# Attention probabilities of two heads handled together: the row shift, the cast and where they stand in each engine's queue

## The chip, the cores and the metric

The kernel runs on one core of a Trainium2 chip. A core has five engines that work side by side, each through its own queue and strictly in order: TensorE (PE in the profile, its weight loads PEld), VectorE (DVE), ScalarE (ACT), GpSimd (POOL) and SyncE (SP), which here only issues DMAs. The metric is the device time of one execution in microseconds (us), the median of several runs.

## The reference

The input x is 2048 rows of 576. Each row is normalised (`_layernorm`), and two branches use the result xn. The first is causal attention with a window of 256 over 32 heads of 18 columns each:

```python
qkv = (xn @ wqkv)                       # 3 x 32 heads x 18
scores = einsum("bhqd,bhkd->bhqk", q, k) * (18 ** -0.5)
mask = (0 <= q_index - k_index) & (q_index - k_index < 256)
p = softmax(where(mask, scores, -1e9))
s = einsum("bhqk,bhkd->bhqd", p, v) @ wo
```

The second is a bilinear gated block without a nonlinearity inside: g = silu(((xn @ w_gate) * (xn @ w_up)) @ w_down), with an inner width of 4608. The output is x + s * g.

## The kernel before, in words

All products are made in float16 with a high part and a low part: a value v becomes hi = f16(v) and lo = f16(v - hi), and two or three products of the parts replace one. That holds for the attention probabilities too: `probs` makes the high part and `turn_probs` the low one.

A first stage of some 185 us normalises x and makes q, k and v. The long middle stage, from there to about 1540 us, is a loop over 72 slots of 16 places each; a slot is one of 18 groups of 256 inner columns times one of 4 chunks of 512 rows. In every place TensorE makes a quarter of a gate or up product (L896 to L900). Everything else is hung on places by a list written out by hand, `at(slot, place, function)`: at each place the functions are called after the matmuls of the quarter, score products first, then down products, then the others in the order in which they were put on the list. This order is the order in each engine's queue. Places count on past 15 into the next slot, so place 18 of a slot is place 2 of the next.

Step s of the attention (64 of them, four row chunks c by 16 pairs of heads) lives in slot s + 1 and some places of the next. It has four blocks i of 128 rows, and two heads j. `score_pairs` (L647) makes the score tiles of two blocks, at places 3 and 11, into four banks of PSUM. Then, for each block and head:

- `score`: DVE reads the scores from PSUM, adds the mask, writes them to `sm` and takes the row maximum (L655, shown in the trace as a custom instruction and a read of its accumulator). POOL turns the maximum into the shift, mx * sig + shift, with one small instruction per head (L657).
- `probs`, two places later: ACT takes exp with a scale `sig` and the shift, both read from memory (L662), and casts the result to float16 into `pp` (L665).
- `turn_probs`, two more places later: the low part sm - hi is made by DVE for head 0 and by POOL for head 1 (L670). With head 1 the pair is complete, and SP issues one DMA that transposes `pp` into `pt` (L673).
- `weigh` (L682): TensorE multiplies `pt` with v.

For the first 16 steps (c = 0) the blocks i = 0, 1, 2, 3 have 128, 256, 384, 384 columns of scores per head, later ones 384 throughout.

The other users of DVE in a slot, in the order of the queue: the eviction of each half tile of the down product, `down` (L770 on PE, then L775 on DVE). There are eight of them in a slot, at places 7, 9, 11, 13, 15, 17, 19 and 21, and all use the one bank `dn`, so that a product can start only when the one before it is evicted. Then `up_out` (L747), `h_lo` (L757), the low parts of the weights `up_lo` and `dn_lo` (both L150), and the maxima of the raw weights (L356). At place 12 of every slot stands `finish` of the step before (its place 28): DVE divides the attention output (L694, L696, L698), and POOL casts it and makes its low part (L702, L706). GpSimd also makes a third, scaled copy of the down weights, `dn_low` (L394), twice in four slots.

The low parts of the weights at place 13, between the evictions of places 13 and 15, stand in two of every four slots (`up_lo` at 45 and `dn_lo` at 61, counted from the start of the group).

Of the kernel before, what the change touches and what calls it, by code (L numbers as in the profile page):

```python
# [8 lines left out]
F32 = mybir.dt.float32  # L9
FR = mybir.dt.float32r  # L10
BF = mybir.dt.bfloat16
F16 = mybir.dt.float16
AF = mybir.ActivationFunctionType
OP = mybir.AluOpType
# [6 lines left out]
def kernel(  # L21
# [10 lines left out]
    nc = tc.nc  # L32
# [12 lines left out]
    scale = DH ** -0.5  # L45
    shift = 14.0 * math.log(2.0)
# [11 lines left out]
    G_SC, U_SC, LO = 2.0 ** -27, 2.0 ** -17, 2.0 ** 11  # L58
# [27 lines left out]
    sig = const.tile([128, 4], F32, name="sig")  # L86
# [304 lines left out]

    def dn_low(g, k):
        w = DW[g, k]
        nc.gpsimd.tensor_scalar(w[:, 2], w[:, 0], 1.0 / LO, None, op0=OP.mult)  # L394


    def v_store(t):
# [35 lines left out]
    a, b = TB.pop(0)  # L433
# [87 lines left out]
    for t in range(16):  # L521
# [17 lines left out]
        elif t in (3, 5):  # L539

            k = (t + 5) // 2 - 1
# [11 lines left out]
        for m in range(QM):  # L553
            for c in (2 * half, 2 * half + 1):
# [6 lines left out]
                if half == 1:  # L561
                    if m in (1, 2, 3):
                        ffn_amax(0, m - 1, c - 2)
                    if m >= QM - 2:
                        k = 2 * (m - QM + 2) + c - 2
# [36 lines left out]
    att = att_stack.enter_context(tc.tile_pool(name="att", bufs=1))  # L602
    bias = att.tile([128, 384], BF, name="bias")
# [5 lines left out]
    QS, KS, VT, SP, SM, PP, PT, PVB, OB = {}, {}, {}, {}, {}, {}, {}, {}, {}  # L609
# [27 lines left out]
    def first_kb(s):  # L637
        return 2 if s < 16 else 0
# [11 lines left out]
    def score(s, j, i):  # L650
        ps = SP.pop((s, j, i))
        n = (i + 3 - max(first_kb(s), i)) * 128
        sm = att.tile([128, 384], F32, name="sm_", bufs=4)
        mx = att.tile([128, 2], F32, name="mx", bufs=3)
        nc.vector.tensor_tensor_reduce(sm[:, 384 - n:], ps[:, :n], bias[:, 384 - n:], 1.0, -3e38,  # L655
                                       op0=OP.add, op1=OP.max, accum_out=mx[:, 0:1])
        nc.gpsimd.tensor_scalar(mx[:, 1:2], mx[:, 0:1], sig[:, 1:2], shift, op0=OP.mult, op1=OP.add)  # L657
        SM[s, j, i] = (sm[:, 384 - n:], mx, n)

    def probs(s, j, i):  # L660
        sm, mx, n = SM[s, j, i]
        nc.scalar.activation(sm, sm, AF.Exp, bias=mx[:, 1:2], scale=sig[:, 0:1])  # L662
        if j == 0:
            PP[s, i] = att.tile([128, 1536], F16, name="pp", bufs=3)
        nc.scalar.copy(PP[s, i][:, 2 * n * j:2 * n * j + n], sm)  # L665

    def turn_probs(s, j, i):
        sm, mx, n = SM.pop((s, j, i))
        pp, a = PP[s, i], 2 * n * j
        (nc.gpsimd if j else nc.vector).tensor_tensor(pp[:, a + n:a + 2 * n], sm, pp[:, a:a + n], op=OP.subtract)  # L670
        if j == 1:
            pt = PT[s, i] = att.tile([128, 12, 128], F16, name="pt", bufs=3)
            nc.sync.dma_start(pt[:, 0:4 * n // 128], PP.pop((s, i))[:, 0:4 * n], transpose=True)  # L673

    def weigh(s, j, i):
        if (j, i) == (0, 0):
# [40 lines left out]
    def at(slot, place, f, *a):  # L717
        todo.setdefault(slot * 16 + place, []).append((f, a))

    first_slot = 1  # L720
    for s in range(NSTEP):
        b = first_slot + s
        at(b - 1, 5, load_k, s)
        at(b - 1, 9, load_q, s)
        at(b - 1, 13, load_v, s)
        at(b, 3, score_pairs, s, 0)
        at(b, 11, score_pairs, s, 2)
        for n in range(8):
            i, j = divmod(n, 2)
            p = (3, 4, 6, 8, 11, 12, 14, 16)[n]  # L730
            at(b, p, score, s, j, i)
            at(b, p + 2, probs, s, j, i)
            at(b, p + 4, turn_probs, s, j, i)
            at(b, 15 + 4 * i + (j if i < 3 else 0), weigh, s, j, i)
        at(b, 28, finish, s)
        if s % 16 == 15:
            for i in range(4):
                at(b, 33 + 4 * i, store_o, s // 16, i)
# [38 lines left out]
    for g in range(NG):  # L777
        b = 4 * g - 4
        if g > 0:
            for kind in range(3):  # L780
                for part in range(2):
                    at(b, ((0, 1, 2, 6, 10, 14) if g == 1 else (-6, -2, 2, 6, 10, 14))[2 * kind + part],
                       ffn_raw, g, kind, part)
                for half in range(2):
                    at(b, ((9, 13) if g == 1 else (5, 9), (17, 21), (24, 26))[kind][half], ffn_amax, g, kind, half)
            at(b, 28, ffn_spread_out, g)
            at(b, 34, ffn_spread_in, g)
            at(b, 41, ffn_scale, g)
            for k, (ph, pl) in enumerate(((42, 45), (47, 49), (51, 53), (55, 57))):
                at(b, ph, up_hi, g, k)  # L790
                at(b, pl, up_lo, g, k)
        for k, (ph, pw, pl) in enumerate(((60, 62, 61), (64, 66, 66)) if g else ((64, 65, 66), (68, 69, 70))):
            at(b, ph, dn_hi, g, k)
            at(b, pw, dn_low, g, k)
            at(b, pl, dn_lo, g, k)
# [89 lines left out]
    for sl in range(NSLOT + 1):  # L885
        g, c = divmod(sl, NCH)
        for place in range(16):
            if sl < NSLOT:
                k, quarter = divmod(place, 4)
                up, w = k % 2, UW[g, k]  # L890
# [3 lines left out]
                for i in range((13 * quarter + 3) // 4, (13 * (quarter + 1) + 3) // 4):  # L894
                    a, b = pl[i]
# [44 lines left out]
```

## Time and profile before

| quantity | value |
|---|---|
| median of 3 runs | 1655.34 us (1654.82 to 1655.62) |
| profiled execution, first to last instruction | 1651.6 us |
| granted TensorE clock, mean | 1.000 |
| busy PE / DVE / ACT / POOL | 1638.3 / 1185.1 / 913.6 / 596.2 us |
| share of the chain that ended last: PE | 93% |

The profiled execution gives only the span between its first and its last instruction; the difference to the median, 3.7 us, is what lies around it. A row of the timeline gives the start and the duration in us, the engine, the line, the operation, and what is written and read; in brackets is the idle time of the engine before it and who ended it. On one engine the next instruction often starts some 0.08 us before the end that is shown for the one before it. Where a duration per instruction is wanted as a step in a queue, the distance from start to start is therefore the right one. A row of the groups gives count, total busy time, mean in ns, and idle time before.

### The profile page before, as it was taken

Reading aid. Unit: us, or ns where it says so; the run is one execution under the profiler, and the core shown is the slowest. Engines: PE = TensorE matmul, PEld = TensorE weight load, DVE = VectorE, ACT = ScalarE, POOL = GpSimd, SP = SyncE. Lnnn points to the kernel's source line nnn. Section 1 sums busy time; section 2 is a strip of 40 time slices with the busy share of each in tenths; the row PEclk is TensorE's granted clock in tenths of the full one; section 3 lists DMA queues with packets and bytes.
Section 4 is the critical chain, followed back from the end, with each engine's and each line's share of the span. In section 5 each row is a group of like instructions: output and inputs, shape, how many; then the busy total and the mean of one; then the engine's idle time right before and its main releaser. Section 6 shows DMA issues by size and latency. Waiting matters only on the chain.

```text
span 1651.6 us, 33875 instructions
## 1 busy us (share of the span) xinstructions
PE 1638.3 (99%) x12307; PEld 933.2 (56%) x12307; DVE 1185.1 (72%) x2985; ACT 913.6 (55%) x1578; POOL 596.2 (36%) x1043
## 2 busy tenths in 40 slices
PE   8999999999999999999999999999999999999999
PEld 5464455555555555555555555555555555555577
DVE  7533577777777878787878777878787787865544
ACT  6431465656565666676666666665666666632230
POOL 3110134445343535454444444444444443511000
PEclk9999999999999999999999999999999999999999
DMA  9482445455556766665666575757665656650228
GB/s 239 134 216 90 116 84 115 90 114 104 114 106 132 142 124 135 109 146 112 145 135 142 105 147 105 151 105 145 138 135 113 140 116 129 126 123 28 60 69 219
DMA packets 535079, 206.39 MB, mean 125 GB/s; under 512 B 473856, under 2 KB 513664, under 8 KB 534912
## 3 DMA queue, kind: packets, MB, share of 16 engines
q1 hardware_dynamic: 534912, 204.23, 57.8%
q8 instruction: 97, 1.59, 0.4%
q14 instruction: 70, 0.57, 0.1%
HBM read 76.63 MB, written 23.75 MB: 61 GB/s over the span
## 4 chain that ended last, share of the span: by engine, by line
PE 93%; DMA 3%; DVE 1%; SPq 1%; POOL 1%; issue 1%; ACT 0%; POOLq 0%; ACTq 0%
PE up L896 47%; PE dn L770 25%; PE up L323 5%; PE pv L682 4%; PE up L899 3%; PE s L647 2%; DMA pt<-pp 2%; PE s L860 2%; PE up L860 1%; PE s L291 1%; PE s L770 1%; PE up L291 1%; SPq L337 1%; DMA xr<-in_A_x_dram 0%; SPq L238 0%
## 5 line engine op out<-in xcount | busy, mean ns | idle before, releaser
L896 PE MATMUL up<-XT,upw 128*128 128x512 f16 x3744 | 926.8, 378 | 0.0
L770 PE MATMUL dn<-dnw,hh 128*128 128x288 f16 x3360 | 504.5, 286 | 0.0
L896 PEld LDWEIGHTS <-upw 128*128 128x128 f16 x3744 | 331.1, 97 | 279.6 <-issue 0.6
L775 DVE SCALAR_TENSOR_TENSOR acc<-dn,sc,acc 128x288 f32<-128x288 f32 x528 | 272.2, 516 | 285.9 <-PE dn L770 285.8
L770 PEld LDWEIGHTS <-hh 128*128 128x128 f16 x3456 | 326.1, 98 | 199.0 <-issue 41.1
L657 POOL TENSOR_SCALAR mx<-mx,sig 128x1 f32<-128x1 f32 x512 | 193.5, 378 | 551.3 <-DVE mx L655 526.2
L682 PEld LDWEIGHTS <-pt 128*128 128x128 f16 x2880 | 137.3, 96 | 62.9 <-DMA pt<-pp 5.2
L682 PE MATMUL pv<-vt,pt 128*128 128x37 f16 x2880 | 143.0, 179 | 2.9 <-DMA pt<-pp 2.9
L742 ACT ACTIVATE gt<-up 128x512 f32<-128x512 f32 x144 | 85.4, 593 | 84.5 <-PE up L899 81.4
L752 ACT ACTIVATE hh<-ht 128x512 f16<-128x512 f32 x144 | 89.9, 624 | 61.5 <-DVE ht L747 61.5
L747 DVE SCALAR_TENSOR_TENSOR ht<-up,gt 128x512 f32<-128x512 f32 x144 | 99.0, 688 | 16.6 <-PE up L896 6.6
L757 DVE SCALAR_TENSOR_TENSOR hh<-hh,ht 128x512 f16<-128x512 f16 x144 | 98.7, 685 | 0.0
L323 PE MATMUL up<-XT,upw 128*128 128x512 f16 x448 | 97.0, 379 | 0.0
L356 DVE TENSOR_REDUCE am<-raw 128x1 f32<-128x640 f32 (+1 forms) x108 | 85.0, 787 | 3.0 <-DMA raw<-in_B_w_gate_dram 3.0
L394 POOL TENSOR_SCALAR dnw<-dnw 128x576 f16<-128x576 f16 x36 | 69.1, 1921 | 23.0 <-ACT dnw L147 20.3
L147 ACT ACTIVATE upw<-raw,sc 128x640 f16<-128x640 f32 x72 | 59.2, 824 | 26.1 <-DVE sc L126 26.1
L323 PEld LDWEIGHTS <-upw 128*128 128x128 f16 x448 | 43.8, 98 | 52.5
L328 DVE SCALAR_TENSOR_TENSOR qp<-up,qp 128x512 f16<-128x512 f32 x36 | 24.7, 685 | 59.4 <-ACT qp L327 42.7
L150 DVE SCALAR_TENSOR_TENSOR upw<-raw,sc,upw 128x640 f16<-128x640 f32 x72 | 63.1, 876 | 0.1
L647 PE MATMUL s<-ks,qs 54*128 54x384 f16 (+2 forms) x512 | 60.2, 312 | 0.0
L327 ACT ACTIVATE qp<-up 128x512 f16<-128x512 f32 x36 | 21.4, 597 | 66.6 <-PE up L323 56.1
L899 PE MATMUL up<-XT,upw 64*128 64x512 f16 x144 | 55.7, 387 | 0.0
(2227 smaller groups left out, 2123.1 us busy)
## 6 DMA issues: line engine op xcount, KB each, us to landing
raw<-in_B_w_down_dram SPq DMA_DIRECT2D x36, 288.0 KB
raw<-in_B_w_gate_dram SPq DMA_DIRECT2D x36, 256.0 KB
raw<-in_B_w_up_dram SPq DMA_DIRECT2D x36, 256.0 KB
qk_d<-qp SPq DMA_DIRECT2D x112, 72.0 KB
vt<-v_d SPq DMA_DIRECT2D x48, 111.0 KB
ks<-qk_d SPq DMA_DIRECT2D x96, 54.0 KB
v_d<-vo SPq DMA_DIRECT2D x16, 296.0 KB
xr<-in_A_x_dram SPq DMA_DIRECT2D x16, 288.0 KB
```

The source lines that it names most:

```text
L323: nc.tensor.matmul(ps, a, b, start=i == 0, stop=i == len(pl) - 1)
L647: nc.tensor.matmul(ps[:, :hi_ - lo_], QS[s][r, i * 128:(i + 1) * 128], KS[s][r, lo_:hi_], start=True, stop=True)
L657: nc.gpsimd.tensor_scalar(mx[:, 1:2], mx[:, 0:1], sig[:, 1:2], shift, op0=OP.mult, op1=OP.add)
L682: nc.tensor.matmul(PVB[s][:, j, i, :VW], pt[:, 2 * nb * j + n], VT[s][:, lo_ + n % nb, j * VW:(j + 1) * VW], start=n == 0, stop=n == 2 * n ...
L742: nc.scalar.activation(g, ps, AF.Copy, scale=G_SC)
L747: nc.vector.scalar_tensor_tensor(h, ps, U_SC, GT.pop((sl, ft)), op0=OP.mult, op1=OP.mult)
L752: nc.scalar.activation(hh[:, 0], h, AF.Copy, scale=1.0 / LO)
L757: nc.vector.scalar_tensor_tensor(hh[:, 1], hh[:, 0], -LO, h, op0=OP.mult, op1=OP.add)
L770: nc.tensor.matmul(ps[:, :HALF], a, b, start=q == 0, stop=q == len(l) - 1)
L775: nc.vector.scalar_tensor_tensor(d, ps[:, :HALF], SC[g][:, 9:10], d, op0=OP.mult, op1=OP.add)
L896: nc.tensor.matmul(banks[up], a, b, start=i == 0 and not up, stop=i == 12 and up == 1)
L899: nc.tensor.matmul(banks[0], *half_pass(w, c, False), start=False, stop=True)
```

## The change

For each block, both heads now share one `sm` and one `mx` tile. The DVE instruction multiplies by -C (the value `sig[:, 1:2]`, read from memory) while it adds the mask, and takes the minimum in place of the maximum, so that its accumulator already holds the scaled shift without its constant. POOL adds the constant for both heads with one instruction. `probs` and `turn_probs` are called once per block, at the places that head 1 had: two exps with the constant scale -1, one cast for both heads, then both low parts and the transposition. So head 0's exp, cast and low part move: its low part on DVE from places 7, 10, 15 and 18 to 8, 12, 16 and 20. The pools have three buffers of two heads where `sm` had four of one. The third copy of the down weights is written with a second operation, a multiplication by 1.0.

```diff
-        nc.gpsimd.tensor_scalar(w[:, 2], w[:, 0], 1.0 / LO, None, op0=OP.mult)
+        nc.gpsimd.tensor_scalar(w[:, 2], w[:, 0], 1.0 / LO, 1.0, op0=OP.mult, op1=OP.mult)
...
     def score(s, j, i):
-        sm = att.tile([128, 384], F32, name="sm_", bufs=4)
-        mx = att.tile([128, 2], F32, name="mx", bufs=3)
-        nc.vector.tensor_tensor_reduce(sm[:, 384 - n:], ps[:, :n], bias[:, 384 - n:], 1.0, -3e38,
-                                       op0=OP.add, op1=OP.max, accum_out=mx[:, 0:1])
-        nc.gpsimd.tensor_scalar(mx[:, 1:2], mx[:, 0:1], sig[:, 1:2], shift, op0=OP.mult, op1=OP.add)
+        if j == 0:
+            SM[s, i] = (att.tile([128, 2, 384], F32, name="sm_", bufs=3), att.tile([128, 4], F32, name="mx", bufs=3), n)
+        sm, mx, n = SM[s, i]
+        nc.vector.tensor_tensor_reduce(sm[:, j, :n], ps[:, :n], bias[:, 384 - n:], sig[:, 1:2], 3e38,
+                                       op0=OP.add, op1=OP.min, accum_out=mx[:, j:j + 1])
+        if j == 1:
+            nc.gpsimd.tensor_scalar(mx[:, 2:4], mx[:, 0:2], 1.0, shift, op0=OP.mult, op1=OP.add)
 
-    def probs(s, j, i):
-        nc.scalar.activation(sm, sm, AF.Exp, bias=mx[:, 1:2], scale=sig[:, 0:1])
-        nc.scalar.copy(PP[s, i][:, 2 * n * j:2 * n * j + n], sm)
+    def probs(s, i):
+        for j in range(2):
+            nc.scalar.activation(sm[:, j, :n], sm[:, j, :n], AF.Exp, bias=mx[:, 2 + j:3 + j], scale=-1.0)
+        PP[s, i] = att.tile([128, 2, 2, 384], F16, name="pp", bufs=3)
+        nc.scalar.copy(pp_of(s, i)[:, :, 0], sm[:, :, :n])
 
-    def turn_probs(s, j, i):
-        (nc.gpsimd if j else nc.vector).tensor_tensor(pp[:, a + n:a + 2 * n], sm, pp[:, a:a + n], op=OP.subtract)
-        if j == 1:
-            nc.sync.dma_start(pt[:, 0:4 * n // 128], PP.pop((s, i))[:, 0:4 * n], transpose=True)
+    def turn_probs(s, i):
+        for j in range(2):
+            (nc.gpsimd if j else nc.vector).tensor_tensor(pp[:, j, 1], sm[:, j, :n], pp[:, j, 0], op=OP.subtract)
+        nc.sync.dma_start(pt[:, 0:4 * n // 128], PP.pop((s, i)).rearrange("p j k n -> p (j k n)")[:, 0:4 * n], transpose=True)
...
             at(b, p, score, s, j, i)
-            at(b, p + 2, probs, s, j, i)
-            at(b, p + 4, turn_probs, s, j, i)
+            if j == 1:
+                at(b, p + 2, probs, s, i)
+                at(b, p + 4, turn_probs, s, i)
```

More of the change, by code (lines that the diff above doesn't have):

```diff
@@ L652, in score @@
         n = (i + 3 - max(first_kb(s), i)) * 128
-        sm = att.tile([128, 384], F32, name="sm_", bufs=4)
-        mx = att.tile([128, 2], F32, name="mx", bufs=3)
-        nc.vector.tensor_tensor_reduce(sm[:, 384 - n:], ps[:, :n], bias[:, 384 - n:], 1.0, -3e38,
-                                       op0=OP.add, op1=OP.max, accum_out=mx[:, 0:1])
-        nc.gpsimd.tensor_scalar(mx[:, 1:2], mx[:, 0:1], sig[:, 1:2], shift, op0=OP.mult, op1=OP.add)
-        SM[s, j, i] = (sm[:, 384 - n:], mx, n)
@@ L660, in probs @@
-    def probs(s, j, i):
-        sm, mx, n = SM[s, j, i]
-        nc.scalar.activation(sm, sm, AF.Exp, bias=mx[:, 1:2], scale=sig[:, 0:1])
-        if j == 0:
-            PP[s, i] = att.tile([128, 1536], F16, name="pp", bufs=3)
-        nc.scalar.copy(PP[s, i][:, 2 * n * j:2 * n * j + n], sm)
-    def turn_probs(s, j, i):
-        sm, mx, n = SM.pop((s, j, i))
-        pp, a = PP[s, i], 2 * n * j
-        (nc.gpsimd if j else nc.vector).tensor_tensor(pp[:, a + n:a + 2 * n], sm, pp[:, a:a + n], op=OP.subtract)
-        if j == 1:
-            pt = PT[s, i] = att.tile([128, 12, 128], F16, name="pt", bufs=3)
-            nc.sync.dma_start(pt[:, 0:4 * n // 128], PP.pop((s, i))[:, 0:4 * n], transpose=True)
+        if j == 0:
+            SM[s, i] = (att.tile([128, 2, 384], F32, name="sm_", bufs=3), att.tile([128, 4], F32, name="mx", bufs=3), n)
@@ new lines, in score @@
+        sm, mx, n = SM[s, i]
+        nc.vector.tensor_tensor_reduce(sm[:, j, :n], ps[:, :n], bias[:, 384 - n:], sig[:, 1:2], 3e38,
+                                       op0=OP.add, op1=OP.min, accum_out=mx[:, j:j + 1])
+        if j == 1:
+            nc.gpsimd.tensor_scalar(mx[:, 2:4], mx[:, 0:2], 1.0, shift, op0=OP.mult, op1=OP.add)
+    def probs(s, i):
+        sm, mx, n = SM[s, i]
+        for j in range(2):
+            nc.scalar.activation(sm[:, j, :n], sm[:, j, :n], AF.Exp, bias=mx[:, 2 + j:3 + j], scale=-1.0)
+        PP[s, i] = att.tile([128, 2, 2, 384], F16, name="pp", bufs=3)
+        nc.scalar.copy(pp_of(s, i)[:, :, 0], sm[:, :, :n])
@@ new lines, in pp_of @@
+    def pp_of(s, i):
+        n = SM[s, i][2]
+        return PP[s, i].rearrange("p j k n -> p (j k n)")[:, :4 * n].rearrange("p (j k n) -> p j k n", j=2, k=2)
+    def turn_probs(s, i):
+        sm, mx, n = SM[s, i]
+        pp = pp_of(s, i)
+        for j in range(2):
+            (nc.gpsimd if j else nc.vector).tensor_tensor(pp[:, j, 1], sm[:, j, :n], pp[:, j, 0], op=OP.subtract)
+        del SM[s, i]
+        pt = PT[s, i] = att.tile([128, 12, 128], F16, name="pt", bufs=3)
+        nc.sync.dma_start(pt[:, 0:4 * n // 128], PP.pop((s, i)).rearrange("p j k n -> p (j k n)")[:, 0:4 * n], transpose=True)
```

## The prediction

> **What bounds the kernel now.** I read the busy shares first, then the chain of work that ended last, then the waits of PE, and last the timeline of single slots.
>
> ```profile
> span 1651.6 us, 33875 instructions
> PE 1638.3 (99%) x12307; PEld 933.2 (56%) x12307; DVE 1185.1 (72%) x2985; ACT 913.6 (55%) x1578; POOL 596.2 (36%) x1043
> ```
> ```profile
> 304.67 1.52 PE up L896 x7
> 324.03 1.52 PE up L896 x7
> ...
> 517.79 1.52 PE up L896 x7
> 537.62 1.52 PE up L896 x7
> ...
> 1453.77 1.52 PE up L896 x7
> ```
> ```profile
> PE pv L682 <- DMA pt<-pp: 2.9, 5, 0.9
> ```
>
> PE works 99% of the span. In the chain, the same piece of a slot comes back every 19.36 us in the early attention steps (324.03 - 304.67) and every 19.83 us in the later ones (537.62 - 517.79). Over the 47 slots from 517.79 to 1453.77 that makes 47 x 19.826 = 931.8 us against 936.0 measured. So only 4.2 us of lateness lie in the late slots, and the one wait that PE shows there is `weigh` on the transposed probabilities. This bounds any gain: relieving POOL or ACT can return at most 4.2 us. A loss has no such bound, because each wait that PE gets in a slot is paid up to 64 times. So the question is which wait of PE is nearest. It is that of a down product for the bank `dn`.
>
> ```profile
> 1213.67 0.52 DVE L775 SCALAR_TENSOR_TENSOR acc<-dn,sc,acc 128x288 f32<-128x288 f32 x1 [1.08 <-PE dn L770]
> 1214.10 0.55 DVE L655 CUSTOM_DVE_ANT_0 sm__17557<-s,bias 128x384 f32<-128x384 f32 x1
> ...
> 1214.57 0.69 DVE L757 SCALAR_TENSOR_TENSOR hh<-hh,ht 128x512 f16<-128x512 f16 x1
> 1215.17 0.20 DVE L694 RECIPROCAL rc<-pv 128x8 f32<-128x8 f32 x1
> 1215.29 0.47 DVE L696 TENSOR_REDUCE o<-pv 128x72 f32<-128x144 f32 x2
> 1215.80 0.31 DVE L698 TENSOR_TENSOR o<-o,rc 128x144 f32<-128x144 f32 x1
> 1216.02 0.55 DVE L655 CUSTOM_DVE_ANT_0 sm__17578<-s,bias 128x384 f32<-128x384 f32 x1
> ...
> 1216.50 0.51 DVE L775 SCALAR_TENSOR_TENSOR acc<-dn,sc,acc 128x288 f32<-128x288 f32 x1
> ...
> 1218.68 0.55 DVE L670 TENSOR_TENSOR pp<-sm__17557,pp 128x384 f16<-128x384 f32 x1
> 1219.14 0.55 DVE L655 CUSTOM_DVE_ANT_0 sm__17647<-s,bias 128x384 f32<-128x384 f32 x1
> ```
> ```profile
> 1212.72 0.91 PE L770 MATMUL dn<-dnw,hh 128*128 128x288 f16 x6
> ...
> 1215.28 0.90 PE L770 MATMUL dn<-dnw,hh 128*128 128x288 f16 x6
> ...
> 1217.31 0.90 PE L770 MATMUL dn<-dnw,hh 128*128 128x288 f16 x6
> ```
>
> The down products of places 11, 13 and 15 start at 1212.72, 1215.28 and 1217.31. DVE evicts the first as soon as it ends (1212.72 + 0.91 = 1213.63, start 1213.67) and runs without a gap until the second is evicted, at 1216.50 + 0.51 = 1217.01. The third product starts at 1217.31. The margin is 0.30 us, and nothing in front of it on DVE is idle: 3.34 us of work from 1213.67 to 1217.01.
>
> **The change part by part.**
>
> *The low part of head 0, on DVE.* For block i = 1 it moves from place 10 to place 12, thus from in front of the eviction of place 11, where DVE idled 1.08 us, to between `finish` (L698) and the score instruction of i = 2: into the chain just shown. Its step in the queue is 1219.14 - 1218.68 = 0.46 us.
>
> *The scale read from memory.* All 512 score instructions get it, two of them in this chain. No score instruction of before has it. Nearest rows:
>
> ```profile
> L775 DVE SCALAR_TENSOR_TENSOR acc<-dn,sc,acc 128x288 f32<-128x288 f32 x528 | 272.2, 516 | 285.9 <-PE dn L770 285.8
> L747 DVE SCALAR_TENSOR_TENSOR ht<-up,gt 128x512 f32<-128x512 f32 x144 | 99.0, 688 | 16.6 <-PE up L896 6.6
> ```
>
> Both read PSUM. The time per element comes from the low parts of 384 and 256 columns (0.55 above, 0.42 below, so about 1.02 ns): L775, with a scale from memory, keeps 516 - 294 = 222 ns beside its elements, L747, with a constant, 688 - 522 = 166. So I take 0.06 us each; the ends are 0 and twice that (0.12).
>
> *Sum in the chain, late slots.* 0.46 + 2 x 0.06 = 0.58 us more. A release takes some 0.05 us (PE's end to DVE's start above is 0.04). PE is late by 0.58 - 0.30 + 0.05 = **0.33 us in each of 48 late slots**: 15.8 us. In every fourth slot one more DVE instruction stands in the chain and takes about 0.07 of the margin (0.18, of which 0.1 overlaps): 12 x 0.07 = 0.8.
>
> ```profile
> L361 DVE TENSOR_TENSOR am<-am 128x3 f32<-128x3 f32 x18 | 3.2, 176 | 0.0
> ```
>  In the 15 early slots that have both a `finish` and a block i = 1, the low part has 256 columns:
>
> ```profile
> 380.89 0.42 DVE L670 TENSOR_TENSOR pp<-sm__4670,pp 128x256 f16<-128x256 f32 x1
> ```
>
> That is a step of 0.33, so 0.33 + 0.12 - 0.30 + 0.05 = 0.20 each, with L361's share 3.3 us. Together **20 us**. Nothing gives it back: PE is full, and DVE starts its next chain only at the next product of place 11.
>
> *A collision of DVE and POOL behind it.* Half of the slots (32) have a low part of weights (L150) after the eviction of place 13.
>
> ```profile
> 1117.25 0.51 DVE L775 SCALAR_TENSOR_TENSOR acc<-dn,sc,acc 128x288 f32<-128x288 f32 x1
> 1117.68 0.81 DVE L150 SCALAR_TENSOR_TENSOR dnw<-raw,sc,dnw 128x576 f16<-128x576 f32 x1
> ...
> 1119.48 0.51 DVE L775 SCALAR_TENSOR_TENSOR acc<-dn,sc,acc 128x288 f32<-128x288 f32 x1
> ...
> 1122.09 1.18 DVE L670 TENSOR_TENSOR pp<-sm__16066,pp 128x384 f16<-128x384 f32 x1
> ```
> ```profile
> 1116.92 0.30 POOL L702 CAST ob<-o 128x144 f16<-128x144 f32 x1 [0.78 <-DVE o L698]
> 1117.31 0.46 POOL L706 TENSOR_TENSOR ob<-o,ob 128x144 f16<-128x144 f32 x1
> 1117.73 1.54 POOL L670 TENSOR_TENSOR pp<-sm__15950,pp 128x384 f16<-128x384 f32 x1
> ...
> 1121.95 0.91 POOL L670 TENSOR_TENSOR pp<-sm__16038,pp 128x384 f16<-128x384 f32 x1
> ```
> ```profile
> 1120.61 0.90 PE L770 MATMUL dn<-dnw,hh 128*128 128x288 f16 x6
> ...
> 1123.38 0.91 PE L770 MATMUL dn<-dnw,hh 128*128 128x288 f16 x6
> ```
>
> POOL's low part takes 0.91 alone. Started 0.05 behind DVE's L150, it takes 1.54: it does its work after 1118.49, when L150 has ended. DVE's low part takes 0.55 alone, and 1.18 when it starts 0.14 behind POOL's. So the one that comes first holds the other, if both DVE inputs lie in SBUF. After the change L150 comes 0.58 later, at 1118.26. POOL's L702 comes while DVE makes the moved low part (1116.83 to 1117.38) and is held to about 1117.6; L706 follows, and POOL's low part of i = 1 runs from about 1118.1 to 1119.0. Now POOL is first. L150 ends at about 1119.7 in place of 1119.07: 0.6 more. The eviction of place 15, at 1119.99 before, ends 0.58 + 0.06 + 0.6 later, at 1121.2, where place 17's product (1120.61) would start at 1120.94: **0.35 us in 32 slots, 11 us**. Were L702 not held, POOL's low part would end at 1118.7 and this term would fall to about 0.05.
>
> The Trainium skill states this lock as a rule (SBUF — State Buffer, "Who interferes with whom"): VectorE with two SBUF inputs contends with GpSimd's reads, and issue order decides who blocks. The two rows agree; by the rule L702 too is held and the sum has these 11 us, and if the engines ran side by side it would lack them.
>
> *ACT.*
>
> ```profile
> L662 ACT ACTIVATE sm__2150<-sm__2150,mx,sig x1: 707/707/707, 209.7 to 209.7; 128x384 f32<-128x384 f32 x1
> ...
> L665 ACT CAST pp<-sm__2037 x1: 298/298/298, 201.6 to 201.6; 128x128 f16<-128x128 f32 x1
> ...
> L665 ACT CAST pp<-sm__2150 x1: 512/512/512, 210.4 to 210.4; 128x384 f16<-128x384 f32 x1
> ```
>
> The casts give 0.84 ns per element, so a cast of 768 takes 0.83. An exp with one operand from memory less takes 0.61 (bounds 0.5 to 0.71). After the last score instruction the chain is two exps and one cast, 2.0 us, where it was 1.2. For i = 2 the shift waits for POOL's low part of i = 1 (1119.0 above), so the cast ends near 1121.4. DVE waits there for 0.3 to 1.6 us, with the eviction of place 17 queued behind it. That still ends near 1122.9, and place 19's product is due at 1123.38 + 0.33. I cost the wait at nothing, with 0.7 us of cover; if the chain were 0.9 longer, PE would pay 0.2 in each slot. For the other blocks the cast is ready when DVE comes, within 0.3 us.
>
> *POOL.*
>
> ```profile
> L657 POOL TENSOR_SCALAR mx<-mx,sig 128x1 f32<-128x1 f32 x512 | 193.5, 378 | 551.3 <-DVE mx L655 526.2
> L394 POOL TENSOR_SCALAR dnw<-dnw 128x576 f16<-128x576 f16 x36 | 69.1, 1921 | 23.0 <-ACT dnw L147 20.3
> ```
>
> 256 of 512 small instructions go, 97 us of a third-busy engine. The third copy in its new form has no row; 36 of them at 1.4 (POOL's 0.91 for 384 columns, scaled to 576) to 2.0 us save 19 us or cost 3, beside PE. I take 0 for both. The transposition of i = 1 still waits for `finish` on POOL: its last input is ready 0.3 later in plain slots, as late as PE is, and 0.3 earlier in slots with L150 (1119.0 against 1119.27), where PE is also later. About half of the 4.2 us goes: -2. SP's order of DMAs is unchanged.
>
> Sum: 1651.6 + 20 + 11 - 2 = 1680.6 for the profiled span. The median of the runs shown lies 3.7 above the span, so 1684.
>
> **The rivals.**
>
> 1. The collision does not come out that way (L702 is not held, or L150 still comes first): 1655.3 + 20 = 1675. The order of starts, 1118.1 against 1118.26, is close.
> 2. The scale from memory costs nothing: 0.21 and 0.08 per slot, 12 us in all with L361; without collision and waits on transpositions, 1655 + 12 - 4 = 1663, else up to 1670. L655 is another instruction than L775, which speaks for it.
> 3. The moved low part is held by POOL in turn, 0.27 us or more (1.18 against 0.55 in the row above): 63 x 0.27 = 17 us more, 1701. Against it: POOL's cast is released by L698 too, and starts 0.15 behind DVE's next instruction.
> 4. Not slower: if the chain from place 11 to place 13 grows by less than 0.25 us, no product waits, and the shift that no longer stands on POOL before block 1's low part removes the waits on transpositions: 1655.3 - 4.2 = 1651. The 0.46 of the moved instruction alone speaks against it; it would have to run beside something.
> 5. The change does not relieve what bounds: POOL's 97 us and ACT's savings move nothing. That is part of each case above but the fourth.
>
> **How the numbers follow.** Forecast (20 + 11 - 2) 0.50, rival one 0.20, rival two 0.12, rival three 0.13, rival four 0.05. The predicted time is the first case's, 1684; its own range, with 0.2 to 0.45 for the collision and 0.05 around the scale, is 1676 to 1692. The range from 1662 to 1704 takes in the bounds of cases two and three and leaves out case four and tails, 0.15 in all. Only case four is faster; a measurement of this kernel tells 0.2% (3.3 us) from no change. Faster 0.04, same 0.02, slower 0.94.
>
> **What would show it.** PE gets a new wait, the down product (L770 before) on DVE's eviction, 0.2 to 0.4 us in nearly every slot, and a second one in half of them; a late slot lasts 20.2 or 20.5 us in place of 19.83. The score instruction takes 0.61 us for 384 columns. L150 lasts about 1.4 us where POOL comes first. DVE shows idle time before the low part of i = 2, ended by ACT's cast. POOL's busy time falls by about 100 us or more and the time does not follow. The prediction is wrong if evictions stay 0.2 us ahead of the products, or if the new waits of PE are on `pt` or on the scores' banks.

## The result and the profile after

The changed kernel takes **1683.4 us** (median of 4 runs, 1681.8 to 1684.1) against 1655.4 us before (4 runs beside it): the ratio is 1.0172, with a 95% interval of 1.0157 to 1.0186. It is slower by 28 us. The profiled execution took 1684.1 us and spans 1682.4 us, 30.8 more than the profile before.

In every run on record the time is 1.7 to 1.8 us above the span. So the profile of before, with its span of 1651.6, is of an execution that took about 1653.3 (an estimate from these two numbers), 2.1 below its median, while the profile of after lies 0.7 above its median. Of the 30.8 us, some 2.8 thus lie in which executions were profiled, and 28.0 in the change. The 3.7 us that were put around the span before are 1.7 and this 2.0. One execution of one kernel below (block 1 apart, weights later) took 3403 us, twice as long as its ten others; nothing on record explains it, and its ratio leaves it out.

The head of the page, with the span, the busy times and the first line of the chain that ended last:

```profile
span 1682.4 us, 33363 instructions
...
PE 1654.4 (98%) x12307; PEld 934.4 (56%) x12307; DVE 1232.9 (73%) x2985; ACT 801.2 (48%) x1322; POOL 442.8 (26%) x787
...
PE 76%; DVE 17%; issue 3%; DMA 2%; SPq 1%; POOL 0%; ACT 0%; DVEq 0%; POOLq 0%
```

ACT works 112 us less and POOL 153 us less, and the time went up all the same. PE was 93% of the chain before; now DVE is 17% of it. The waits of PE, DVE and POOL (who waits, for whom, total us, count, longest):

```profile
POOL pp L676 <- ACT pp L666: 239.3, 129, 2.1
...
DVE pp L676 <- ACT pp L666: 55.6, 63, 1.5
...
PE dn L777 <- DVE acc L782: 13.7, 52, 1.1
```

The last row is new: the down product waits for DVE's eviction of the bank `dn`. Its 13.7 us are not the whole lateness: in the slot shown below the wait is recorded with 0.19 us where the product is 0.36 late. So the starts of the 560 down products on `dn` in this trace are compared with those of before, interval by interval, and the excess of each interval is added up over all slots. I call the excess between the products of places 13 and 15 the **first wait**, and that between places 15 and 17 the **second wait**.

| piece of the 30.8 us | predicted | measured |
|---|---|---|
| first wait | 20 | 23.5, in 63 slots |
| second wait | 11 | 8.0, in 31 slots |
| intervals in which `weigh` waited on `pt` (places 7 to 9, 19 to 21) | -2 | -3.6 |
| first stage and rest | 0 | 2.9 |

Of the last row, 1.6 us lie before the first down product and 1.2 in a single slot.

The timeline of one slot shows both waits, in the same places as the chain that the prediction showed of before. L782 is the eviction, L676 the low part, L708 POOL's cast of `finish`, L656 the score reduction.

```profile
1278.81 0.52 DVE L782 SCALAR_TENSOR_TENSOR acc<-dn,sc,acc 128x288 f32<-128x288 f32 x1 [0.84 <-PE dn L777]
1279.24 0.61 DVE L656 CUSTOM_DVE_ANT_0 sm__17305<-s,bias,sig 128x384 f32<-128x384 f32 x1
...
1280.42 0.90 PE L777 MATMUL dn<-dnw,hh 128*128 128x288 f16 x6
...
1281.23 0.55 DVE L676 TENSOR_TENSOR pp<-sm__17194,pp 128x384 f16<-128x384 f32 x1
1281.38 0.56 POOL L708 CAST ob<-o 128x144 f16<-128x144 f32 x1 [2.98 <-DVE o L704]
1281.70 0.61 DVE L656 CUSTOM_DVE_ANT_0 sm__17305<-s,bias,sig 128x384 f32<-128x384 f32 x1
...
1282.24 0.52 DVE L782 SCALAR_TENSOR_TENSOR acc<-dn,sc,acc 128x288 f32<-128x288 f32 x1
1282.45 0.91 POOL L676 TENSOR_TENSOR pp<-sm__17194,pp 128x384 f16<-128x384 f32 x1
1282.67 1.37 DVE L150 SCALAR_TENSOR_TENSOR upw<-raw,sc,upw 128x640 f16<-128x640 f32 x1
1282.81 0.90 PE L777 MATMUL dn<-dnw,hh 128*128 128x288 f16 x6 [0.19 <-DVE acc L782]
...
1285.10 0.50 DVE L782 SCALAR_TENSOR_TENSOR acc<-dn,sc,acc 128x288 f32<-128x288 f32 x1
...
1285.66 0.90 PE L777 MATMUL dn<-dnw,hh 128*128 128x288 f16 x6
...
1286.14 0.56 DVE L676 TENSOR_TENSOR pp<-sm__17305,pp 128x384 f16<-128x384 f32 x1 [0.54 <-ACT pp L666]
```

From the first row to the end of the second eviction (1282.24 + 0.52 = 1282.76) DVE has work without a gap, as before, but the work is 3.95 us long in place of 3.34. The product of place 15 starts at 1282.81, 0.05 after the eviction's end, and so 2.39 us after the one of place 13 (1280.42), where it was 2.03. Then L150 stands behind POOL's low part, which came first by 0.22 us, and takes 1.37; the eviction of place 15 ends at 1285.60 and place 17's product starts at 1285.66, 2.85 us after the one before it in place of 2.56.

### The profile page after: what moved, and what is told of

Its sections match the earlier page's. It is cut to its first block, busy times and chain, and to the rows that moved or that the text cites. A ratio compares the mean times of both kernels' runs of the same rounds, so it can differ in the third digit from the quotient of the medians.

```text
span 1682.4 us, 33363 instructions
## 1 busy us (share of the span) xinstructions
PE 1654.4 (98%) x12307; PEld 934.4 (56%) x12307; DVE 1232.9 (73%) x2985; ACT 801.2 (48%) x1322; POOL 442.8 (26%) x787
## 3 DMA queue, kind: packets, MB, share of 16 engines
q8 instruction: 97, 1.59, 0.4%
## 4 chain that ended last, share of the span: by engine, by line
PE 76%; DVE 17%; issue 3%; DMA 2%; SPq 1%; POOL 0%; ACT 0%; DVEq 0%; POOLq 0%
PE up L903 34%; PE dn L777 22%; PE up L323 5%; DVE acc L782 3%; PE up L906 3%; PE pv L688 3%; PE s L647 2%; DVE hh L764 2%; DVE pp L676 2%; PE s L867 2%; DVE o L702 1%; PE s L291 1%; PE up L867 1%; DVE ht L754 1%; PE up L291 1%
## 5 line engine op out<-in xcount | busy, mean ns | idle before, releaser
L777 PE MATMUL dn<-dnw,hh 128*128 128x288 f16 x3360 | 504.2, 286 | 17.5 <-DVE acc L782 13.7
L782 DVE SCALAR_TENSOR_TENSOR acc<-dn,sc,acc 128x288 f32<-128x288 f32 x528 | 270.3, 512 | 217.1 <-PE dn L777 217.0
L764 DVE SCALAR_TENSOR_TENSOR hh<-hh,ht 128x512 f16<-128x512 f16 x144 | 115.8, 804 | 0.0
L659 POOL TENSOR_SCALAR mx<-mx 128x2 f32<-128x2 f32 x256 | 62.5, 244 | 191.1 <-DVE mx L656 175.6
L708 POOL CAST ob<-o 128x144 f16<-128x144 f32 x64 | 33.4, 521 | 301.1 <-DVE o L704 291.3
L356 DVE TENSOR_REDUCE am<-raw 128x1 f32<-128x640 f32 (+1 forms) x108 | 84.6, 784 | 2.7 <-DMA raw<-in_B_w_gate_dram 2.7
L150 DVE SCALAR_TENSOR_TENSOR upw<-raw,sc,upw 128x640 f16<-128x640 f32 x72 | 69.5, 966 | 0.1
L906 PE MATMUL up<-XT,upw 64*128 64x512 f16 x144 | 55.7, 387 | 0.0
L907 PE MATMUL up<-XT,upw 64*128 64x512 f16 x144 | 55.6, 386 | 0.0
```

Source lines behind the costliest of these rows:

```text
L356: nc.vector.tensor_reduce(SC[g, "am"][:, half, kind:kind + 1], r, axis=AX.X if kind == 2 else AX.XY, op=OP.max, apply_absolute_value=True)
L764: nc.vector.scalar_tensor_tensor(hh[:, 1], hh[:, 0], -LO, h, op0=OP.mult, op1=OP.add)
L777: nc.tensor.matmul(ps[:, :HALF], a, b, start=q == 0, stop=q == len(l) - 1)
L782: nc.vector.scalar_tensor_tensor(d, ps[:, :HALF], SC[g][:, 9:10], d, op0=OP.mult, op1=OP.add)
L906: nc.tensor.matmul(banks[0], *half_pass(w, c, False), start=False, stop=True)
```

## The experiments

Each kernel is the kernel before or the changed kernel with the edit shown; line numbers shift with the edits. All compute the whole result. Each ratio is taken against executions of the kernel before that ran beside that kernel (medians of 1652.5 to 1655.4 us). The waits are found as above, in us over all slots:

| kernel | time, us | ratio to before | first wait | second wait |
|---|---|---|---|---|
| changed kernel | 1683.4 | 1.0172 | 23.5 | 8.0 |
| old copy form | 1682.3 | 1.0171 | 23.4 | 8.1 |
| constant scale again | 1676.3 | 1.0137 | 16.7 | 8.1 |
| weights' low parts later | 1676.0 | 1.0136 | 23.4 | -0.1 |
| low part of block 1 at place 10 | 1676.7 | 1.0139 | 12.3 | 12.6 |
| the same, second row maximum earlier | 1668.3 | 1.0082 | 4.9 | 12.6 |
| all three of these moves | 1665.2 | 1.0072 | 10.1 | -0.1 |
| block 1 apart | 1662.1 | 1.0060 | 0 | 11.4 |
| block 1 apart, weights later | 1655.3 | 1.0015 | 0 | 0 |
| before, low part of block 1 moved | 1675.8 | 1.0132 | 16.1 | 8.5 |
| before, scale from memory | 1664.2 | 1.0061 | 0 | 11.4 |
| before, scale from memory, weights later | 1652.7 | 0.9991 | 0 | 0 |
| before, new copy form | 1653.7 | 0.9998 | - | - |

The intervals of the ratios are 0.0008 to 0.0017 to either side.

### One part of the change alone

The **moved low part** alone, in the kernel before (n counts block and head, n = 2 is block 1, head 0):

```diff
-            at(b, p + 4, turn_probs, s, j, i)
+            at(b, 12 if n == 2 else p + 4, turn_probs, s, j, i)
```

> The kernel before, with one thing changed: DVE's low part of head 0 of block 1 at place 12 in place of 10. Scale, shift, exps, casts and the copy stay as they were. Theory: 0.46 - 0.30 + 0.05 = 0.21 us in late slots, 0.08 in early ones, some 0.2 more where L361 stands in the chain, 14 us in all; plus up to 8 us where POOL's low part now comes before the low part of the weights; minus up to 3 us of waits on transpositions: 1666 to 1676. Rival A (late casts): 1655, since the casts are as before.

Measured: 1675.8 us, inside. PE is late by 0.23 us in late slots, 0.48 where L361 stands in the chain, and 0.09 in early ones, 16.1 us together; the second wait comes with it, 8.5 us. So this one move brings most of the loss: no joined cast, no shift for two heads and no scale from memory is needed for it. In one late slot with `upw`:

```profile
1275.53 0.55 DVE L670 TENSOR_TENSOR pp<-sm__18046,pp 128x384 f16<-128x384 f32 x1
...
1276.48 0.51 DVE L775 SCALAR_TENSOR_TENSOR acc<-dn,sc,acc 128x288 f32<-128x288 f32 x1
1276.75 0.91 POOL L670 TENSOR_TENSOR pp<-sm__18088,pp 128x384 f16<-128x384 f32 x1
1276.91 1.44 DVE L150 SCALAR_TENSOR_TENSOR upw<-raw,sc,upw 128x640 f16<-128x640 f32 x1
1277.04 0.90 PE L770 MATMUL dn<-dnw,hh 128*128 128x288 f16 x6
```

The product starts 0.05 us after the end of the eviction, and L150 is again behind POOL.

The **scale from memory** alone, in the kernel before, heads apart:

```diff
-                                       op0=OP.add, op1=OP.max, accum_out=mx[:, 0:1])
+                                       op0=OP.add, op1=OP.min, accum_out=mx[:, 0:1])
```

and with it the operand `sig[:, 1:2]` and the initial value 3e38 in the line above, the factor 1.0 in POOL's instruction and -1.0 in the exp, as the change has them.

> The kernel before with the scale of the score instruction read from memory (minimum, constant scale -1 in exp), heads apart and every instruction at its old place. Theory: the chain between the evictions of places 11 and 13 grows by 0.12 us, under its margin of 0.25, so PE does not see it: 1651 to 1656. If 0.06 us per score instruction counted by itself, 512 x 0.06 = 31 us more: 1685.

Measured: 1664.2 us, a miss by 8 us. The first wait is indeed 0: the margin only shrinks. But the second wait is there with 11.4 us in 32 slots, and DVE is late there through a lost race:

```profile
1105.15 0.46 POOL L706 TENSOR_TENSOR ob<-o,ob 128x144 f16<-128x144 f32 x1
1105.57 0.91 POOL L670 TENSOR_TENSOR pp<-sm__15638,pp 128x384 f16<-128x384 f32 x1
1105.58 1.59 DVE L150 SCALAR_TENSOR_TENSOR upw<-raw,sc,upw 128x640 f16<-128x640 f32 x1
```

POOL starts 0.01 us ahead of L150, and L150 takes 1.59 us. Before, L150 started at 1117.68, 0.05 us ahead of POOL's 1117.73, and took 0.81 (rows in the prediction, there for `dnw`). In the trace of before L150 is 0.05 or 0.06 us ahead in all 32 such slots; here POOL is 0.01 us ahead, or level with it, in all 32. A reduction that is 0.06 us longer turned that around.

To test the race, the same kernel with the weights' low parts behind the score reduction that follows them:

```diff
-            for k, (ph, pl) in enumerate(((42, 45), (47, 49), (51, 53), (55, 57))):
+            for k, (ph, pl) in enumerate(((42, 46), (47, 49), (51, 53), (55, 57))):
...
-        for k, (ph, pw, pl) in enumerate(((60, 62, 61), (64, 66, 66)) if g else ((64, 65, 66), (68, 69, 70))):
+        for k, (ph, pw, pl) in enumerate(((60, 62, 62), (64, 66, 66)) if g else ((64, 65, 66), (68, 69, 70))):
```

> The kernel before with the constant exp scale replaced by the changed kernel's scale from memory and row minimum (heads still apart), which alone took 1664.2 us, and besides the low parts of the weights' chunks moved from place 13 to place 14, behind the score reduction of the next block. Theory that the loss of that kernel is only the race of the weights' low part (L150) against GpSimd's low part of block 1, won by 0.05 us before and lost by 0.01 us with the slower reductions: the weights' low part now meets nothing of GpSimd's, and the time returns to 1651 to 1656 us. Rival, that the 0.06 us which each reduction and each max gets longer costs by itself, by DVE's lateness at every place: it stays at 1662 to 1666 us.

Measured: 1652.7 us, ratio 0.9991 (0.9982 to 0.9999): all of the loss is gone, and in that trace the down products keep the intervals of before, but for single slots. The first two rows are one of the moved low parts and POOL's; the last is a low part of the weights that meets nothing of POOL's:

```profile
1257.53 0.91 POOL L670 TENSOR_TENSOR pp<-sm__18088,pp 128x384 f16<-128x384 f32 x1
...
1258.07 1.06 DVE L150 SCALAR_TENSOR_TENSOR upw<-raw,sc,upw 128x640 f16<-128x640 f32 x1
...
1267.04 0.88 DVE L150 SCALAR_TENSOR_TENSOR upw<-raw,sc,upw 128x640 f16<-128x640 f32 x1
```

The moved low part still meets the end of POOL's, unlike the theory: it starts 0.54 us behind POOL and takes 1.06 in place of 0.88, and no product is later for it. So the longer reduction costs only through the race. This step also tells that the shift formed from the minimum, and the exp with a constant scale, bring no more than 0.1%. The kernel before with the later weights alone was not run; by the 4.2 us of lateness in its late slots, it could hide a cost of no more than that.

The **copy**, from both sides: the changed kernel with the old form, and the kernel before with the new one.

```diff
-        nc.gpsimd.tensor_scalar(w[:, 2], w[:, 0], 1.0 / LO, 1.0, op0=OP.mult, op1=OP.mult)
+        nc.gpsimd.tensor_scalar(w[:, 2], w[:, 0], 1.0 / LO, None, op0=OP.mult)
```

> The changed kernel with the third copy of the down weights in its old form, so 36 instructions of 1.92 us in place of 0.87 on POOL. Theory: the copy is beside every wait of PE, so no change against the changed kernel: 1681 to 1686. If POOL's time counted, up to 38 us / 1683 = 2% slower.

> The kernel before with the third copy in its new form alone. Theory: nothing on PE's path, 1651 to 1655; the most it can return are the 4 us of waits on transpositions.

Measured: 1682.3 (ratio 1.0171 beside 1.0172) and 1653.7 us (0.9998, 0.9989 to 1.0006). The copy is worth nothing on the path, although POOL's 36 copies fall from 69.1 us to 31.3 (row below).

### One part of the change undone

The scale constant again in the changed kernel:

```diff
-        nc.vector.tensor_tensor_reduce(sm[:, j, :n], ps[:, :n], bias[:, 384 - n:], sig[:, 1:2], 3e38,
-                                       op0=OP.add, op1=OP.min, accum_out=mx[:, j:j + 1])
+        nc.vector.tensor_tensor_reduce(sm[:, j, :n], ps[:, :n], bias[:, 384 - n:], 1.0, -3e38,
+                                       op0=OP.add, op1=OP.max, accum_out=mx[:, j:j + 1])
```

(and `sig` back in POOL's instruction and in the exp.)

> The changed kernel with the score instruction's scale a constant again: maximum in place of minimum, POOL multiplies by sig and adds the shift for both heads in its one instruction, exp reads its scale from memory again. Theory: the chain has 2 x 0.06 us less, 63 slots, so 7.5 us less than the changed kernel: about 1676. Rival A (late casts): each pair of exps is 0.2 longer, the cast later, so slower than the changed kernel, 1688 or more. If the scale costs nothing in the chain: 1683.

Measured: 1676.3 us. The first wait falls from 23.5 to 16.7; 6.8 us over 63 slots are 0.108 each, two reductions of 0.054. The second wait stays at 8.1.

The weights' low parts at place 14, in the changed kernel (the edit shown above):

> The changed kernel with the low parts of the weights of place 13 moved to place 14, behind the score instruction of block 3 on DVE. Theory: the chain is as long as in the changed kernel, but the low part of the weights then meets only the end of POOL's low part, so the second wait of PE (31 slots, 8 us in the trace) goes and the first stays: about 1675. Rival B (the lock is the whole cost): about 1655. Rival A (late casts): no difference, 1683.

Measured: 1676.0 us. The second wait is gone (8.0 to -0.1) and the first is untouched. A smaller one comes elsewhere, 2.1 us between the products of places 5 and 7.

The moved low part back at place 10:

```diff
+    def low0(s, i):
+        sm, mx, n = SM[s, i]
+        pp = pp_of(s, i)
+        nc.vector.tensor_tensor(pp[:, 0, 1], sm[:, 0, :n], pp[:, 0, 0], op=OP.subtract)
+
...
-        for j in range(2):
-            (nc.gpsimd if j else nc.vector).tensor_tensor(pp[:, j, 1], sm[:, j, :n], pp[:, j, 0], op=OP.subtract)
+        nc.gpsimd.tensor_tensor(pp[:, 1, 1], sm[:, 1, :n], pp[:, 1, 0], op=OP.subtract)
...
+                at(b, p + 2 if i == 1 else p + 4, low0, s, i)
                 at(b, p + 4, turn_probs, s, i)
```

> The changed kernel, but DVE's low part of head 0 of block 1 is made at place 10, in front of the eviction of place 11, where DVE idles; exps, cast, POOL's low part and the transposition stay where the change put them. Theory (the moved instruction lengthens DVE's chain between the evictions of places 11 and 13): the chain is then only 0.12 us longer than before, under its margin of 0.25, and both terms go, 1652 to 1660 us; what may be left is the low part waiting for the cast and pushing the eviction of place 11 by up to 0.2. Rival A (one late cast for two heads makes DVE wait and PE pays for that): the cast is as late as in the changed kernel and DVE waits for it here too, 1680 us or more. Rival B (only the lock between DVE and POOL costs): 1675, since the low part stands no longer in POOL's way.

Measured: 1676.7 us, a miss by 17 us. It is near rival B's number but not for rival B's reason, since the second wait grows. With one cast for both heads, the low part at place 10 has to wait for it. In one slot of four a row maximum of the raw weights (L356) and then the eviction stand behind it:

```profile
1251.95 0.56 DVE L675 TENSOR_TENSOR pp<-sm__16911,pp 128x384 f16<-128x384 f32 x1 [1.31 <-ACT pp L666]
1252.42 0.74 DVE L356 TENSOR_REDUCE am<-raw 128x1 f32<-128x576 f32 x1
1253.09 0.51 DVE L787 SCALAR_TENSOR_TENSOR acc<-dn,sc,acc 128x288 f32<-128x288 f32 x1
...
1256.67 0.90 PE L782 MATMUL dn<-dnw,hh 128*128 128x288 f16 x6 [0.70 <-DVE acc L787]
```

The first wait is 0.85 us in the mean of these 12 slots (0.38 to 1.00) and at most 0.09 in the others, 12.3 us; the second wait is 12.6, since POOL is first there too, by 0.01 us in all 32 slots.

With that row maximum a place earlier:

```diff
-                    at(b, ((9, 13) if g == 1 else (5, 9), (17, 21), (24, 26))[kind][half], ffn_amax, g, kind, half)
+                    at(b, ((9, 13) if g == 1 else (5, 9), (17, 21), (24, 25))[kind][half], ffn_amax, g, kind, half)
```

> The changed kernel with VectorE's low part of block 1 back at place 10 (1676.7 us by itself) and besides the second row maximum of w_down at place 9 instead of place 10, so that it does not stand behind the low part while that waits for its cast. Theory that the 12.3 us which the first wait still lost there, all of it in the one slot of four with that row maximum, came from this queueing: about 10 to 12 us go, 1664 to 1668 us remain, and what remains is the second wait (12.6 us, L150 beside GpSimd's low part). Rival, that a low part at place 10 that waits for the one late cast delays the eviction whatever stands between: 1674 to 1678 us, as without the step.

Measured: 1668.3 us, 0.3 above what the theory gave; the first wait fell from 12.3 to 4.9. The queue behind the low part is most of that wait, not all of it: 0.24 us in the mean stay in the slots that have L361 in the chain, and 0.08 in half of the others.

All three moves at once (low part at place 10, weights later, row maximum earlier):

> The changed kernel with the three places put right that the earlier runs showed: DVE's low part of head 0 of block 1 at place 10, the low parts of the weights of place 13 at place 14, and the second maximum of the down weights at place 9 in place of 10, so that it does not stand behind the low part that waits for the cast. Theory: the first wait falls to at most 0.08 us in half of the late slots (2 us), the second goes, the waits on transpositions stay small: 1651 to 1656, the time of the kernel before or a little less. If another wait of the one cast for two heads is hidden behind the two that were seen: 1660 or more.

Measured: 1665.2 us, a miss by 9 us. The second wait is gone, but a first wait of 0.30 us stands in two slots of four (and 0.20 to 0.36 in the third kind), 10.1 us, and 4.9 us more lie between places 5 and 7, in those same two slots of four. The trace of one such slot:

```profile
972.10 0.92 POOL L680 TENSOR_TENSOR pp<-sm__13001,pp 128x384 f16<-128x384 f32 x1 [0.93 <-ACT pp L666]
...
972.14 1.42 DVE L769 SCALAR_TENSOR_TENSOR hh<-hh,ht 128x512 f16<-128x512 f16 x1
...
974.49 0.51 DVE L787 SCALAR_TENSOR_TENSOR acc<-dn,sc,acc 128x288 f32<-128x288 f32 x1
...
975.05 0.90 PE L782 MATMUL dn<-dnw,hh 128*128 128x288 f16 x6
...
977.20 1.13 DVE L675 TENSOR_TENSOR pp<-sm__13102,pp 128x384 f16<-128x384 f32 x1
...
980.40 0.83 ACT L666 CAST pp<-sm__13147 128x768 f16<-128x768 f32 x1
...
981.27 0.56 DVE L675 TENSOR_TENSOR pp<-sm__13147,pp 128x384 f16<-128x384 f32 x1 [1.25 <-ACT pp L666]
981.74 0.51 DVE L787 SCALAR_TENSOR_TENSOR acc<-dn,sc,acc 128x288 f32<-128x288 f32 x1
```

and the same slot in the kernel just above, without the later weights, where the first wait is 0.08:

```profile
978.00 0.92 POOL L680 TENSOR_TENSOR pp<-sm__13002,pp 128x384 f16<-128x384 f32 x1 [0.93 <-ACT pp L666]
...
978.50 0.98 DVE L769 SCALAR_TENSOR_TENSOR hh<-hh,ht 128x512 f16<-128x512 f16 x1
...
980.40 0.51 DVE L787 SCALAR_TENSOR_TENSOR acc<-dn,sc,acc 128x288 f32<-128x288 f32 x1
...
981.17 0.90 PE L782 MATMUL dn<-dnw,hh 128*128 128x288 f16 x6
...
983.12 1.12 DVE L675 TENSOR_TENSOR pp<-sm__13102,pp 128x384 f16<-128x384 f32 x1
```

In both, one cast releases both low parts of block 0, they meet, and DVE's takes 1.13 or 1.12 us; that alone is therefore not what made the first wait of 0.30. The difference lies before it. With the later weights `h_lo` starts 0.04 us behind POOL's low part of block 3 and takes 1.42; without them it starts 0.50 behind and takes 0.98. The eviction that follows ends 0.05 us before the product of place 7 in the one, and 0.26 before it in the other. These 0.21 us of lateness then go through block 0, the reductions, the exps and the one cast of block 1, and the low part at place 10 waits for that cast. This reads two slots side by side; no run took the meeting with `h_lo` away by itself.

### Block 1 alone undone

The last two kernels keep the change but put block 1 back to one shift, one cast and one low part per head (head 0 at place 10); the second of them has the weights' low parts at place 14 too. The edit's other lines, the functions for one head and the shift, are not shown.

```diff
...
+            if i == 1:
+                at(b, p + 2, probs1, s, j)
+                at(b, p + 4, turn_probs if j else low0, s, i)
+            elif j == 1:
-            if j == 1:
                 at(b, p + 2, probs, s, i)
+                at(b, p + 4, low0, s, i)
                 at(b, p + 4, turn_probs, s, i)
```

> The changed kernel with only block 1 put back to heads apart (a shift, a cast and a call of the low part for each head, VectorE's low part at place 10 again); the other three blocks stay joined, the scale stays in memory. Theory that the whole first wait came from joining block 1 and that the second wait is the race of the weights' low part against GpSimd's: no first wait, 10 to 12 us of second wait as in the kernel before with the scale from memory alone, 1662 to 1667 us. Rival, that the late cast of the other blocks delays evictions as well: 1670 us or more.

> As the other kernel of this pair, with the low parts of the weights' chunks at place 14 in place of 13 besides. The theory puts both causes out of the way, with three quarters of the joined instructions kept: 1651 to 1656 us, no difference to the kernel before. Rival, that the joined blocks cost by themselves: 1659 us or more, by as much as the other kernel stands above 1665.

Measured: 1662.1 and 1655.3 us. Without the joining of block 1 there is no first wait, and the second is 11.4 us, as with the scale alone. With the race out of the way as well, 0.15% remain (ratio 1.0015, 1.0005 to 1.0024). They stand between places 5 and 7, 3.7 us in 24 slots, where POOL's low part of the joined block 3 meets `h_lo`:

```profile
1266.45 0.92 POOL L689 TENSOR_TENSOR pp<-sm__17456,pp 128x384 f16<-128x384 f32 x1 [2.10 <-ACT pp L668]
...
1266.53 1.38 DVE L781 SCALAR_TENSOR_TENSOR hh<-hh,ht 128x512 f16<-128x512 f16 x1
...
1268.84 0.51 DVE L799 SCALAR_TENSOR_TENSOR acc<-dn,sc,acc 128x288 f32<-128x288 f32 x1
...
1269.40 0.90 PE L794 MATMUL dn<-dnw,hh 128*128 128x288 f16 x6
```

`h_lo` takes 1.38 us where its row before has 0.69, and the product of place 7 starts 0.05 us after the eviction's end. This interval is unchanged (0.0 us) in the changed kernel, with block 1 apart alone, and in the kernel before with the scale and the later weights. In these runs such slots lose time only where casts are joined and the weights come later, so this is no part of the changed kernel's loss. That loss has three parts: block 1's low part in the chain, the scale in the same chain, and the lost race. No version here beats the kernel before by more than 0.1%: PE was full.

## Why the prediction was right, point by point

The groups of the changed kernel that the steps spoke of (count, busy us, mean ns):

```profile
L764 DVE SCALAR_TENSOR_TENSOR hh<-hh,ht 128x512 f16<-128x512 f16 x144 | 115.8, 804 | 0.0
...
L659 POOL TENSOR_SCALAR mx<-mx 128x2 f32<-128x2 f32 x256 | 62.5, 244 | 191.1 <-DVE mx L656 175.6 <-DVE am L361 3.9
...
L394 POOL TENSOR_SCALAR dnw<-dnw 128x576 f16<-128x576 f16 x36 | 31.3, 871 | 23.8 <-ACT dnw L147 21.3
...
L361 DVE TENSOR_TENSOR am<-am 128x3 f32<-128x3 f32 x18 | 4.5, 253 | 0.0
```

- **What bounds the kernel, and the nearest wait**: right. Relieving POOL by 153 us and ACT by 112 returned at most the 3.6 us of waits on `pt`, inside the 4.2 that the prediction set as the bound, and the loss came from the down product on `dn`.
- **The chain, 20 us**: the mechanism holds, the size was 23.5. The low part's step is 0.47 in the slot shown (1281.23 to 1281.70; taken 0.46), the scale 0.054 per reduction (taken 0.06). The chain is 0.61 us longer in that slot, not 0.58; late slots lose 0.35 in place of 0.33 (two odd ones 0.67), early ones 0.22 in place of 0.20. At 0.02 in 48 late slots that is 1.0 of the 3.5 us, and the two odd slots, which have no account here, add 0.6. The term for L361, taken as 0.07, is 0.19 (0.54 against 0.35): it stands beside POOL's work now and takes 0.27 us in the slot shown below (mean 253 ns, before 176). In 12 late slots that is 1.4 us more; the rest, 0.5, is in the early slots.

```profile
1261.87 0.27 DVE L361 TENSOR_TENSOR am<-am 128x3 f32<-128x3 f32 x1
1262.07 0.51 DVE L782 SCALAR_TENSOR_TENSOR acc<-dn,sc,acc 128x288 f32<-128x288 f32 x1
1262.09 0.91 POOL L676 TENSOR_TENSOR pp<-sm__16911,pp 128x384 f16<-128x384 f32 x1
...
1262.63 0.90 PE L777 MATMUL dn<-dnw,hh 128*128 128x288 f16 x6 [0.37 <-DVE acc L782]
```

- **The collision, 11 us**: the mechanism holds, the size was 8.0: 0.20 to 0.31 us per slot in place of 0.35. As predicted, POOL's cast (L702 before, now L708) is held by the moved low part (0.56 us beside 0.30), POOL comes first, and L150 takes 1.37. POOL comes ahead by 0.22 us, not 0.16, so L150 waits less. What the prediction did not draw from the lead of 0.05 us that it had read is that the scale alone, without any moved low part, already loses the race (11.4 us).
- **The rule of the Trainium skill** (SBUF — State Buffer, "Who interferes with whom"), that VectorE with two SBUF inputs contends with GpSimd's reads and that the issue order decides: the runs agree at every meeting shown here, with 0.01 us of lead enough for 1.59 in place of 0.88 us.
- **ACT, costed at nothing**: right for the changed kernel. DVE waits there for ACT's cast (55.6 us in 63 waits, at most 1.5) and no product is later for it. That cover belongs to the place: at place 10 the wait for the cast, with the queue behind it, cost 12.3 us.
- **POOL, taken as 0**: right. The copy in its new form is far cheaper than the 1.4 to 2.0 us taken (871 ns in the mean), and worth nothing.
- **`pt`, -2**: -3.6, nearly the whole 4.2. But with the moved low part alone, where neither POOL's nor ACT's work is cut (592.0 and 913.8 us), the same two intervals are already 2.7 us shorter: PE, late elsewhere, seems to find `pt` ready. How much of the 3.6 came from the relief is not shown. The first stage and the rest, 2.9 us, had no term; nothing in them repeats from slot to slot, and they are as large as the 2.8 us that lie in which executions were profiled.

Of the rivals, the first (no collision) is out by the 8.0 us, the second (scale free) by the 0.054 us in the slot, the third (the low part held by POOL) by the 0.55 us of L676, and the fourth by the first wait. The fifth, that nothing that bounds is relieved, holds as part of the result. That the time was met to 1 us is partly luck: the terms' errors, +3.5, -3.0, -1.6 and +2.9, leave 1.8 us, and the 3.7 us added to the span, of which 2.0 belonged to the profiled execution, made up for them.

## What to carry to other kernels

When one engine is full, do not ask how much work a change takes off the others, but which of their instructions stands between two of its products, and how wide that margin is: here 0.30 us, and a move of two places in a list used it up. Measure also by how little the order of two instructions that hold each other up, on two engines, is decided; 0.05 us of lead decided 11 us over the kernel. Joining two steps into one makes the first of them wait for the second and releases their successors together, so check what is queued behind each one, and whom the released ones now meet.

## What was unexpected of the hardware

- The form of POOL's instruction: multiplying 128x576 float16 by two constants in place of one took 871 ns in the mean, where it had been 1921. Over the runs the means are 700 to 1063 ns in the new form and 1836 to 1921 in the old. Only this one instruction was tried.
- A DVE instruction that meets POOL's low part is held for what is left of it, less 0.14 to 0.19 us: L150 takes 1.59 us for 0.88 when POOL is 0.01 ahead and has 0.90 left, `h_lo` 1.38 for 0.69 with 0.84 left, the low part 1.13 for 0.55 with 0.72 left. So a lead of a hundredth of a microsecond is enough, and it costs more than a clear one: with POOL 0.22 ahead `upw`'s L150 took 1.37.
- An exp over 384 columns with the scale as a constant took 0.61 us (two in 1.12), where it had been 0.71 with the scale read from memory; a reduction that reads its scale from memory took 0.61 in place of 0.55.
